# Linear attention and low-rank mixer on one core: k and v of three batches loaded through ScalarE's queue, alpha and q through SyncE's

## The chip, the cores and the metric

One core of a Trainium2 chip. The metric is the device time of one execution in microseconds. A run is called fast or slow by its own kernel's fastest run: slow is more than 1.5% above it. "SP" is SyncE, "PE" TensorE, "ACT" ScalarE, "DVE" VectorE, "POOL" GpSimd.

## The reference

```python
B, H, S, D = 4, 8, 768, 48
for t in range(S):                      # gated linear attention, per batch and head
    state = alpha[:, :, t, :, None] * state + einsum('bhd,bhe->bhde', k[:, :, t], v[:, :, t])
    y[:, :, t] = einsum('bhd,bhde->bhe', q[:, :, t], state)
x = y.transpose(0, 2, 1, 3).reshape(B, S, 384)
u = x + (x^T @ U @ V)^T                 # mixing over the sequence, rank 32
out = u + relu(u @ w_ch1) @ w_ch2       # 384 -> 1536 -> 384
```

## The kernel before

The kernel is written as a list of operations. A small planner in the kernel's own source (`Plan`) gives each an engine, a cost and a priority, plays the engines forward in time with those costs, and emits every engine's instructions in the order found. Each engine's order is fixed when the program is built. The costs of the plan thus shape the program, but not the chip.

Each batch loads alpha, k, q and v (1.18 MB each, rows of 192 bytes) into six buffers `io`. Sequence chunks of 128 are scanned in pairs: logarithm and cumulated sum of alpha (`lt`, L418 to L425), exponentials `ai` and `aa`, the multiplies `rk` (k, POOL) and `rq` (q, DVE), their transposes `kt` and `qt`, scores (L480), state (L512, L522) and result (L554, L559). For batches 2 and 3 the transposes are DMA transposes issued by SP. Then come the mixer and the two large products (L656, L678), which fill PE between the scans.

```python
def load(b):                                        # cut to the loads of b > 0
    ts = [Buf(io) for _ in range(4)]
    for n, (t, src) in enumerate(zip(ts, (alpha, k, q, v))):
        ...
        op = P.add("SP", 4250, lambda t=t, src=src: nc.sync.dma_start(t()[:, :, 0:D], ...),
                   prio=b + n / 10, hold=800.0, descs=385, late=(0.0, 0.0, 1500.0, 3000.0)[b], ...)
...
# transposes of batches 2 and 3
P.add("SP", 1000, lambda ...: nc.sync.dma_start_transpose(dst()..., src()...), ..., hold=1250.0, land=1300.0, descs=66, late=500.0)
...
# stores
P.add("SP", 550, lambda: nc.sync.dma_start(out[b, c * C : (c + 1) * C, :], ou()), ..., slack=4500.0 if b < 3 else None)
```

The planner's picture of SP (cut from `Plan.run`). Its figures, `RING` = 512 and 850 ns among them, are assumptions of the plan:

```python
free = t
for s, f, n in ring:                                # the plan's limit on queued transfers
    x = sum(m for s2, f2, m in ring if s2 >= s) + op.descs - RING
    if x > 0:
        free = max(free, s + (f - s) * min(1.0, x / n))
clock[eng] = free + op.hold
s = max(dma, clock[eng] + 850.0)                    # the plan's start, 850 ns after the issue
dma = s + op.cost
```

In the plan and in the texts below, "ring" stands for a queue of transfers as the trace lists them: q1 for what SP issues, q10 for what ScalarE issues.

Of the kernel before, what the change touches and what calls it, by code (L numbers as in the profile page):

```python
# [47 lines left out]


RING = 512  # L50
FCOST = 512 / 2.4 + 3.0


class Op:
    __slots__ = ("eng", "cost", "fn", "prio", "deps", "bufs", "n", "end", "users", "est", "i", "hold", "land", "descs", "dma", "slack", "port", "late")


class Plan:
# [9 lines left out]
        self.kinds = {}  # L68
        self.fill, self.fill_fn, self.fill_end, self.banks = None, None, None, ()

    def add(self, eng, cost, fn, r=(), w=(), prio=0.0, after=(), kind=None, hold=450.0, land=550.0, descs=40, dma=None, slack=None, port=False, late=0.0):
        op = Op()
        op.eng, op.cost, op.fn, op.prio = eng, cost, fn, prio
        op.i, op.hold, op.land, op.descs = len(self.ops), hold, land, descs
        op.port, op.late = port, late
        op.dma, op.slack = dma, (self.SLACK if eng == "SP" else 0.0) if slack is None else slack
        op.deps, op.users, op.est, op.end = set(), [], 0.0, None
        for k in r:
            d = self.writer.get(k)
            if d is not None:  # L80
                op.deps.add(d)
        for k in w:
            d = self.writer.get(k)
            if d is not None:
                op.deps.add(d)
            op.deps.update(self.readers.get(k, ()))
        for k in r:
            self.readers.setdefault(k, []).append(op)
        for k in w:
            self.writer[k] = op  # L90
            self.readers[k] = []
        op.deps.update(x for x in after if x is not None)
        if kind is not None:
            if kind in self.kinds:
                op.deps.add(self.kinds[kind])
            self.kinds[kind] = op
        op.deps.discard(op)
        op.bufs = []
        for k in list(r) + list(w):
            b = k[0] if isinstance(k, tuple) else k  # L100
            if isinstance(b, Buf) and b not in op.bufs:
                op.bufs.append(b)
        for b in op.bufs:
            b.left += 1
        self.ops.append(op)
        return op

    def run(self):
# [8 lines left out]
        clock = {"POOL": 1800.0}  # L117
        order = []
        dma = 0.0
        ring = []  # L120
# [3 lines left out]
        while todo:  # L124
            best = None
            for eng, cand in ready.items():
                now = clock.get(eng, 0.0)
                ok = []
                for op in cand:
                    t = op.est  # L130
                    for b in op.bufs:
                        if b.slot is None:
                            s = [f for f in map(b.pool.when, range(len(b.pool.slots))) if f is not None]
                            if not s:
                                t = None
                                break
                            t = max(t, min(s))
                    if t is not None:
                        ok.append((max(t, now), op))
                if not ok:  # L140
                    continue
                t0 = min(t for t, _ in ok)
                t1, op = min(((t, o) for t, o in ok if t <= t0 + 1.0), key=lambda x: (x[1].prio, x[1].i))
                if best is None or t1 < best[0]:
                    best = (t1, eng, op)
            if best is None:
                raise RuntimeError("the plan is stuck")
            t, eng, op = best
# [11 lines left out]
            for b in op.bufs:  # L160
                if b.slot is None:
                    p = b.pool
# [4 lines left out]
            if eng == "SP":  # L167
                free = t
                for s, f, n in ring:
                    x = sum(m for s2, f2, m in ring if s2 >= s) + op.descs - RING  # L170
                    if x > 0:
                        free = max(free, s + (f - s) * min(1.0, x / n))
                clock[eng] = free + op.hold
                s = max(dma, clock[eng] + 850.0)
                dma = s + op.cost
                ring.append((s, dma, op.descs))
                del ring[:-24]
                op.end = dma + op.land
            else:
                other = {"DVE": "POOL", "POOL": "DVE"}.get(eng)  # L180
                if op.port and last.get(other) is not None and last[other].port and clock[other] > t + 150.0:
                    op.cost *= 1.75 if eng == "DVE" else 1.2
                if eng in last:
                    last[eng] = op
                clock[eng] = t + op.cost
                op.end = t + op.cost
                if op.dma is not None:
                    s = max(dma, clock[eng] + 850.0)
                    dma = s + op.dma
                    op.end = dma + op.land  # L190
            order.append((t, op))
# [5 lines left out]
            for u in op.users:  # L197
                u.n -= 1
                lat = 0.0 if u.eng == eng and eng == "PE" else self.LAT[eng]
# [16 lines left out]
def kernel(  # L216
# [12 lines left out]
    nc = tc.nc  # L229
    B, H, S, D = q.shape  # L230
    C = 128
    NC = S // C
# [5 lines left out]
    NCT = DM // 128  # L238
# [10 lines left out]
    P = Plan()  # L249
# [50 lines left out]
    late = banks((0,), (1,), (2,), (3,))  # L300
# [60 lines left out]
    marks = {}  # L361

    def load(b):
        ts = [Buf(io) for _ in range(4)]
        for n, (t, src) in enumerate(zip(ts, (alpha, k, q, v))):
            if b == 0 and n == 2:
                marks["gate"] = P.add("POOL", 36 * 48 * 1.07 + 60, lambda t=t: nc.gpsimd.tensor_copy(t()[:, 0:36, 0:D], ts[0]()[:, 0:36, 0:D]), r=[(ts[0], c) for c in range(NC)], w=[(t, c) for c in range(NC)], prio=2)
            if b == 0 and n in (2, 3):
                for c in range(NC):
                    op = P.add("SP", 950, lambda t=t, src=src, c=c: nc.sync.dma_start(t()[:, :, 0:D].rearrange("p (h c) d -> p c h d", c=NC)[:, c], src[0, :, c * C : (c + 1) * C].rearrange("h p d -> p h d")), w=[(t, c)], prio=0.2 + ({2: (0, 1, 2), 3: (3, 4, 5)})[n][c // 2] / 100 + c / 1000, hold=350.0, descs=65, after=[marks["gate"]], slack=0.0)  # L370
            elif b == 0 and n == 1:
                gate = P.add("POOL", 40 * 48 * 0.9, lambda t=t: nc.gpsimd.memset(t()[:, 0:40, 0:D], 0.0), w=[(t, c) for c in range(NC)], prio=0)
                P.add("ACT", 870, lambda t=t, src=src: nc.scalar.dma_start(t()[:, :, 0:D], src[b].rearrange("h (c p) d -> p (h c) d", p=C)), w=[(t, c) for c in range(NC)], prio=0, after=[gate], dma=4100.0)
            else:
                op = P.add("SP", 4250, lambda t=t, src=src: nc.sync.dma_start(t()[:, :, 0:D], src[b].rearrange("h (c p) d -> p (h c) d", p=C)), w=[(t, c) for c in range(NC)], prio=b + n / 10, hold=800.0, descs=385, after=[marks.get("gate")], late=(0.0, 0.0, 1500.0, 3000.0)[b])
        return ts

    def stage_gla(b, g, sprev, xb, ins):
        kk = b * (NC // G) + g
        pr = 1000 + kk * 10  # L380
# [30 lines left out]
        for i0, n in parts:  # L411
            e = on(ev, i0)
# [29 lines left out]
        for eng, dst, src, fac in ((ek, rk, kt, ai), (eq, rq, qt, aa)):  # L442
            for i0, n in parts if dst is rq else [(0, G)]:
                e = on(eng, i0)
# [13 lines left out]
        both = lambda t: [(t, i) for i in range(G)]  # L458
        for src, dst, eng in ((rk, kT, ekt), (rq, qT, eqt)):
            if b in (2,3):  # L460
                P.add("SP", 1000, lambda src=src, dst=dst: nc.sync.dma_start_transpose(dst().rearrange("p g e c -> p (g e) c"), src().rearrange("t g h w -> t (g h w)")), r=both(src), w=both(dst), prio=pr / 1000 - 1, hold=1250.0, land=1300.0, descs=66, late=500.0)  # L461
                continue
            tb = Buf(gen)
            for i0, n in parts if src is rq else [(0, G)]:
# [120 lines left out]
    def stage_mix(b, xb, uT):  # L585
        pr = 500 + b * 10
# [36 lines left out]
        for c in range(NC):  # L623
# [2 lines left out]
            P.add("DVE", 550, lambda c=c, hb=hb: nc.vector.tensor_tensor(xb()[:, c, :], xb()[:, c, :], hb()[:, 0, 0:DM], op=ALU.add), r=[hb, (xb, c)], w=[(xb, c)], prio=pr)  # L626
            if b in (2,3):
                if c % 3 == 2:
                    P.add("SP", 1100, lambda c=c: nc.sync.dma_start_transpose(uT()[:, c - 2 : c + 1].rearrange("p c j t -> p (c j) t"), xb()[:, c - 2 : c + 1, :].rearrange("p c m -> p (c m)")), r=[(xb, c - i) for i in range(3)], w=[(uT, c // 3, j) for j in range(NCT)], prio=pr / 1000 - 1, hold=1300.0, land=1300.0, descs=66, late=500.0)
                continue  # L630
            if c % 2 == 1:
                ub2 = Buf(gen)
# [38 lines left out]
    def mlp2(b, xb, h1, c, utx):  # L671
# [14 lines left out]
        ou = Buf(outs)  # L686
        P.add("DVE", 550, lambda: nc.vector.tensor_tensor(ou(), xb()[:, c, :], hb()[:, 0, 0:DM], op=ALU.add), r=[hb, (xb, c)], w=[ou], prio=100)  # L687
        if (("SP",)*4)[b] == "SP":
            P.add("SP", 550, lambda: nc.sync.dma_start(out[b, c * C : (c + 1) * C, :], ou()), r=[ou], prio=-1, land=1700.0, slack=4500.0 if b < 3 else None)  # L689
        elif (("SP",)*4)[b] == "POOL":  # L690
            P.add("POOL", 550, lambda: nc.gpsimd.dma_start(out[b, c * C : (c + 1) * C, :], ou()), r=[ou], prio=50, land=2500.0, dma=550.0, slack=4500.0)
        else:
            P.add("ACT", 250, lambda: nc.scalar.dma_start(out[b, c * C : (c + 1) * C, :], ou()), r=[ou], prio=50, land=1700.0, dma=550.0, slack=4500.0)

    P.fill, P.banks = ((0.85, 250.0), (0.6, 700.0)), space
    P.fill_fn = lambda i: nc.tensor.matmul(ps[:, i, 0:512], lhsT=ident, rhs=fill_in, start=True, stop=True)  # L696
# [45 lines left out]
```

## Time and profile before

| | before |
|---|---|
| median of its first three runs | 174.87 us (174.59 to 177.56) |
| span of the profiled run | 173.6 us |
| PE busy, by the page | 157.6 us, so 16.0 us idle |
| of it idle from 30 to 62, and from 62 to 126 us | 0.24 and 8.96 us |
| half-speed spells of PE before the end | one, 3.4 us |
| packets on SP's queue (q1) and ScalarE's (q10) | 31.46 and 1.18 MB |

The idle times are lengths of stretches less PE's busy time in them. A half-speed spell comes from the trace's record of granted clock. It is counted here as half its length, 1.7 us for 3.4, an estimate. Fillers are products without use that keep PE busy. The mean granted clock is 0.987.

The lines themselves are in the prediction below. A timeline line reads: start, length, engine, source line, operation, written tile <- read tile, count, and in brackets the idle time before it with what ended it. "SPq" and "ACTq" lines are DMA issues, whose length is how long the issuing engine was held.

### The profile page before, as it was taken

Reading aid. Unit: us, or ns where it says so; the run is one execution under the profiler, and the core shown is the slowest. Engines: PE = TensorE matmul, PEld = TensorE weight load, DVE = VectorE, ACT = ScalarE, POOL = GpSimd, SP = SyncE. Lnnn points to the kernel's source line nnn. Section 1 sums busy time; section 2 is a strip of 40 time slices with the busy share of each in tenths; the row PEclk is TensorE's granted clock in tenths of the full one; section 3 lists DMA queues with packets and bytes.
Section 4 is the critical chain, followed back from the end, with each engine's and each line's share of the span. In section 5 each row is a group of like instructions: output and inputs, shape, how many; then the busy total and the mean of one; then the engine's idle time right before and its main releaser. Section 6 shows DMA issues by size and latency. Waiting matters only on the chain.

```text
span 173.6 us, 3909 instructions
## 1 busy us (share of the span) xinstructions
PE 157.6 (91%) x1632; PEld 96.3 (55%) x1632; DVE 89.8 (52%) x142; ACT 82.4 (47%) x147; POOL 53.9 (31%) x59
## 2 busy tenths in 40 slices
PE   5997999999999998998766899979799999999992
PEld 2445676556666675665344556536456556656650
DVE  2009991635266823398246128757948643544421
ACT  3296465688848576771533694024342210523200
POOL 8817745507942803247022062800000000000000
PEclk9999999999999999999998799999999999999998
DMA  3999999899998976998986989799400822101122
GB/s 103 274 288 209 192 265 384 254 267 311 372 260 238 260 204 194 251 288 251 208 196 164 251 253 262 187 227 205 124 4 0 186 86 93 46 0 45 54 87 91
DMA packets 58850, 33.14 MB, mean 191 GB/s; under 512 B 31440, under 2 KB 57680, under 8 KB 58832
## 3 DMA queue, kind: packets, MB, share of 16 engines
q1 hardware_dynamic: 56304, 31.46, 66.5%
q10 hardware_dynamic: 1552, 1.18, 2.3%
q0 software_dynamic: 976, 0.25, 1.4%
q8 instruction: 13, 0.21, 0.5%
q14 instruction: 5, 0.04, 0.1%
HBM read 24.08 MB, written 4.72 MB: 166 GB/s over the span
## 4 chain that ended last, share of the span: by engine, by line
PE 50%; DMA 32%; DVE 5%; SPq 5%; POOL 3%; ACT 2%; issue 1%; POOLq 0%; DVEq 0%; ACTq 0%
PE ps L678 19%; PE ps L656 17%; DMA io<-in_v_dram 10%; DMA qt<-rq 8%; DMA io<-in_alpha_dram 7%; DMA io<-in_k_dram 5%; SPq L689 3%; PE ps L451 3%; DVE pm L490 3%; PE ps L480 2%; DMA uT<-xb 2%; PE ps L559 2%; PE ps L696 2%; POOL rv L316 1%; SPq L461 1%
## 5 line engine op out<-in xcount | busy, mean ns | idle before, releaser
L678 PE MATMUL ps<-w_sb,h1t 128*128 128x384 bf16 x288 | 55.2, 326 | 0.0
L656 PE MATMUL ps<-uT,w_sb 128*128 128x384 bf16 x288 | 52.9, 328 | 1.2 <-DMA uT<-xb 1.2
L667 ACT ACTIVATE h1t<-ps 128x384 bf16<-128x384 f32 x48 | 23.5, 492 | 41.2 <-PE ps L656 41.0
L669 DVE TENSOR_SCALAR h1t<-ps 128x384 bf16<-128x384 f32 x48 | 26.3, 555 | 31.1 <-PE ps L656 30.3
L656 PEld LDWEIGHTS <-w_sb 128*128 128x128 bf16 x288 | 27.6, 98 | 18.9 <-DMA uT<-xb 1.5
L678 PEld LDWEIGHTS <-h1t 128*128 128x128 bf16 x288 | 27.5, 98 | 17.8 <-issue 0.6
L440 POOL TENSOR_TENSOR rk<-io,ai 128x768 bf16<-128x768 f32 x10 | 17.3, 1735 | 34.5 <-ACT ai L433 28.0
L490 DVE TENSOR_TENSOR pm<-ps,ut_ones 128x1024 bf16<-128x1024 f32 x18 | 21.6, 1220 | 8.7 <-PE ps L480 8.7
L687 DVE TENSOR_TENSOR ou<-xb,ps 128x384 f32<-128x384 bf16 x24 | 13.3, 553 | 19.9 <-PE ps L678 9.5
L696 PE MATMUL ps<-ones,ident 128*128 128x512 bf16 x52 | 14.5, 416 | 1.9 <-DVE rk L271 1.9
L440 DVE TENSOR_TENSOR rq<-io,aa 128x768 bf16<-128x768 f32 (+1 forms) x11 | 13.1, 1210 | 2.4 <-ACT aa L434 2.3
L575 ACT CAST xb<-ps 128x768 bf16<-128x768 f32 (+1 forms) x15 | 10.0, 672 | 8.0 <-PE ps L559 6.9
L316 POOL CAST rv<-io 128x768 bf16<-128x768 f32 (+1 forms) x11 | 9.7, 910 | 8.0 <-DMA io<-in_v_dram 8.0
L409 ACT ACTIVATE lt<-io 128x768 bf16<-128x768 f32 x12 | 9.8, 843 | 4.3 <-DMA io<-in_alpha_dram 4.0
L433 ACT ACTIVATE ai<-ps 128x768 bf16<-128x768 f32 x12 | 9.8, 817 | 2.7 <-PE ps L420 1.5
L316 POOL CAST w_sb<-io 128x768 bf16<-128x768 f32 x12 | 9.5, 825 | 4.3 <-DMA io<-in_moe_w_ch_dram 4.3
L480 PE MATMUL ps<-qt,kt 48*128 48x128 bf16 x192 | 8.7, 220 | 1.8 <-DMA qt<-rq 1.7
L434 ACT ACTIVATE aa<-ps 128x768 bf16<-128x768 f32 x12 | 9.9, 829 | 0.0
L356 POOL TENSOR_SCALAR_AFFINE_SELECT pm<-pm 128x1024 bf16<-128x1024 bf16 x6 | 6.5, 1092 | 11.0 <-DVE pm L490 8.5
L497 ACT CAST pm<-ps 128x1024 bf16<-128x1024 f32 x6 | 6.0, 1017 | 8.0 <-PE ps L480 8.0
L696 PEld LDWEIGHTS <-ident 128*128 128x128 bf16 x52 | 5.2, 105 | 7.7 <-issue 2.2
L559 PE MATMUL ps<-rv,pm 128*128 128x48 bf16 x192 | 8.5, 187 | 0.9 <-DVE pm L490 0.9
(64 smaller groups left out, 139.3 us busy)
## 6 DMA issues: line engine op xcount, KB each, us to landing
io<-in_moe_w_ch_dram SPq DMA_DIRECT2D x6, 768.0 KB, 7.4
out_dram<-ou SPq DMA_DIRECT2D x24, 192.0 KB, 2.3
io<-in_q_dram SPq DMA_DIRECT2D x6, 192.0 KB, 4.1
io<-in_v_dram SPq DMA_DIRECT2D x6, 192.0 KB, 3.8
vm_sb<-in_moe_V_dram POOLq DMA_DIRECT2D x4, 48.0 KB, 5.8
kt<-rk SPq DMA_TRANSPOSE x6, 2.8
qt<-rq SPq DMA_TRANSPOSE x6, 2.8
io<-in_alpha_dram SPq DMA_DIRECT2D x4, 0.2 KB, 8.6
```

The lines of the kernel that those rows point to most:

```text
L316: ENG[eng].tensor_copy(dst, src)
L440: ENG[eng].tensor_tensor(dst()[:, i0 : i0 + n, :, 0:D], ch(src, i0, n), fac()[:, i0 : i0 + n].rearrange("t g (h d) -> t g h d", d=D), op=A ...
L480: nc.tensor.matmul(s2[:, par, p, :], lhsT=kT()[o : o + D, i, p, :], rhs=qT()[o : o + D, i, p, :], start=(p == 0), stop=(p == HP - 1),)
L490: nc.vector.tensor_tensor(pmi().rearrange("t two hp c -> t (two hp) c"), sc().rearrange("p two (hp c) -> p (two hp) c", c=C), maskc.to_bro ...
L559: nc.tensor.matmul(y2[:, par, p, :], lhsT=pm[i]()[:, par, p, :], rhs=rv()[:, i, 2 * p + par, :], start=s0, stop=s1, skip_group_check=True,)
L575: nc.scalar.copy(x3, y3)
L656: nc.tensor.matmul(hb()[:, 0, 0:TW], lhsT=w1_sb[:, ct, jt * 128 : (jt + 1) * 128], rhs=uT()[:, 3 * tt : 3 * tt + 3, ct, :], start=(ct == 0 ...
L667: P.add("ACT", 500, lambda jt=jt, hb=hb: nc.scalar.activation(h1()[:, jt, :], hb()[:, 0, 0:TW], AF.Relu), r=[hb], w=[(h1, jt)], prio=100)
L669: P.add("DVE", 560, lambda jt=jt, hb=hb: nc.vector.tensor_scalar_max(h1()[:, jt, :], hb()[:, 0, 0:TW], 0.0), r=[hb], w=[(h1, jt)], prio=100)
L678: nc.tensor.matmul(hb()[:, 0, 0:DM], lhsT=h1()[:, jt, (c % 3) * C : (c % 3 + 1) * C], rhs=w2_sb[:, jt, :], start=(jt == 0), stop=(jt == NJ ...
L687: P.add("DVE", 550, lambda: nc.vector.tensor_tensor(ou(), xb()[:, c, :], hb()[:, 0, 0:DM], op=ALU.add), r=[hb, (xb, c)], w=[ou], prio=100)
L696: P.fill_fn = lambda i: nc.tensor.matmul(ps[:, i, 0:512], lhsT=ident, rhs=fill_in, start=True, stop=True)
```

## The change

The intent: SP carries loads, transposes and stores in one queue in the order of their issue, and a load issued soon behind another was seen to hold everything behind it (k of batch 1, issued at 24.66, held SP for 9.45 us; alpha, issued before it at 23.43, landed at 35.43). k and v of batches 1 to 3 go to ScalarE's queue. The planner is given new figures, estimates: 1800 ns from issue to first packet of a load for 850 (1.48 us for q at 66.70 and 1.52 us for v at 102.79 in the trace of the kernel before), SP held until 72% of the last large load has run (v of batch 1 held it until 49.07, 74% of the time from q's first packet at 45.84 to its last at 50.23), 1360 ns for a transpose's issue (1.24 to 1.86 us in that trace). Loads are chained (`pre`), and a ScalarE load may be planned at the earliest 4500 ns (`LEAD`) before the DMA engines are due to be free.

```diff
+LEAD = 4500.0
@@ Plan.run, choice of the next operation
-                    t = op.est
+                    if op.pre is not None and op.pre.end is None:
+                        continue
+                    t = max(op.est, dma - LEAD) if eng == "ACT" and op.dma is not None else op.est
@@ Plan.run, SP
                 clock[eng] = free + op.hold
-                s = max(dma, clock[eng] + 850.0)
+                if ring and ring[-1][2] > 300:
+                    clock[eng] = max(clock[eng], ring[-1][0] + 0.72 * (ring[-1][1] - ring[-1][0]))
+                s = max(dma, clock[eng] + op.lat)
@@ load
+            elif n in ((),(1,3),(1,3),(1,3))[b]:
+                marks["load"] = P.add("ACT", 870, lambda ...: nc.scalar.dma_start(...), ..., dma=4000.0, lat=1800.0, slack=300.0, late=..., pre=marks["load"])
             else:
-                op = P.add("SP", 4250, ..., hold=800.0, descs=385, ...)
+                marks["load"] = P.add("SP", 4000, ..., hold=800.0, descs=385, ..., lat=1800.0, pre=marks.get("load") if b else None)
@@ transposes: cost 1000 or 1100 -> 1250, hold 1250 or 1300 -> 1360 or 1380
@@ stores: slack 4500 -> 3000 for b < 3, lat 1450
```

More of the change, by code (lines that the diff above doesn't have):

```diff
@@ L50 @@
 RING = 512
+LEAD = 4500.0
 FCOST = 512 / 2.4 + 3.0
 class Op:
-    __slots__ = ("eng", "cost", "fn", "prio", "deps", "bufs", "n", "end", "users", "est", "i", "hold", "land", "descs", "dma", "slack", "port", "late")
+    __slots__ = ("eng", "cost", "fn", "prio", "deps", "bufs", "n", "end", "users", "est", "i", "hold", "land", "descs", "dma", "slack", "port", "late", "lat", "pre")
 class Plan:
@@ L69, in __init__, with add @@
         self.fill, self.fill_fn, self.fill_end, self.banks = None, None, None, ()
-    def add(self, eng, cost, fn, r=(), w=(), prio=0.0, after=(), kind=None, hold=450.0, land=550.0, descs=40, dma=None, slack=None, port=False, late=0.0):
+    def add(self, eng, cost, fn, r=(), w=(), prio=0.0, after=(), kind=None, hold=450.0, land=550.0, descs=40, dma=None, slack=None, port=False, late=0.0, lat=850.0, pre=None):
         op = Op()
@@ L74, in add @@
         op.i, op.hold, op.land, op.descs = len(self.ops), hold, land, descs
-        op.port, op.late = port, late
+        op.port, op.late, op.lat = port, late, lat
+        op.pre = pre
         op.dma, op.slack = dma, (self.SLACK if eng == "SP" else 0.0) if slack is None else slack
@@ L187, in run @@
                 if op.dma is not None:
-                    s = max(dma, clock[eng] + 850.0)
+                    s = max(dma, clock[eng] + op.lat)
                     dma = s + op.dma
@@ L373, in load @@
                 P.add("ACT", 870, lambda t=t, src=src: nc.scalar.dma_start(t()[:, :, 0:D], src[b].rearrange("h (c p) d -> p (h c) d", p=C)), w=[(t, c) for c in range(NC)], prio=0, after=[gate], dma=4100.0)
+            elif n in ((),(1,3),(1,3),(1,3))[b]:
+                marks["load"] = P.add("ACT", 870, lambda t=t, src=src: nc.scalar.dma_start(t()[:, :, 0:D], src[b].rearrange("h (c p) d -> p (h c) d", p=C)), w=[(t, c) for c in range(NC)], prio=b + n / 10, dma=4000.0, lat=1800.0, slack=300.0, late=(0.0, 0.0, 1500.0, 3000.0)[b], pre=marks["load"])
             else:
-                op = P.add("SP", 4250, lambda t=t, src=src: nc.sync.dma_start(t()[:, :, 0:D], src[b].rearrange("h (c p) d -> p (h c) d", p=C)), w=[(t, c) for c in range(NC)], prio=b + n / 10, hold=800.0, descs=385, after=[marks.get("gate")], late=(0.0, 0.0, 1500.0, 3000.0)[b])
+                marks["load"] = P.add("SP", 4000, lambda t=t, src=src: nc.sync.dma_start(t()[:, :, 0:D], src[b].rearrange("h (c p) d -> p (h c) d", p=C)), w=[(t, c) for c in range(NC)], prio=b + n / 10, hold=800.0, descs=385, after=[marks.get("gate")], late=(0.0, 0.0, 1500.0, 3000.0)[b], lat=1800.0, pre=marks.get("load") if b else None)
         return ts
@@ L460, in stage_gla @@
             if b in (2,3):
-                P.add("SP", 1000, lambda src=src, dst=dst: nc.sync.dma_start_transpose(dst().rearrange("p g e c -> p (g e) c"), src().rearrange("t g h w -> t (g h w)")), r=both(src), w=both(dst), prio=pr / 1000 - 1, hold=1250.0, land=1300.0, descs=66, late=500.0)
+                P.add("SP", 1250, lambda src=src, dst=dst: nc.sync.dma_start_transpose(dst().rearrange("p g e c -> p (g e) c"), src().rearrange("t g h w -> t (g h w)")), r=both(src), w=both(dst), prio=pr / 1000 - 1, hold=1360.0, land=1300.0, descs=66, late=500.0)
                 continue
@@ L628, in stage_mix @@
                 if c % 3 == 2:
-                    P.add("SP", 1100, lambda c=c: nc.sync.dma_start_transpose(uT()[:, c - 2 : c + 1].rearrange("p c j t -> p (c j) t"), xb()[:, c - 2 : c + 1, :].rearrange("p c m -> p (c m)")), r=[(xb, c - i) for i in range(3)], w=[(uT, c // 3, j) for j in range(NCT)], prio=pr / 1000 - 1, hold=1300.0, land=1300.0, descs=66, late=500.0)
+                    P.add("SP", 1250, lambda c=c: nc.sync.dma_start_transpose(uT()[:, c - 2 : c + 1].rearrange("p c j t -> p (c j) t"), xb()[:, c - 2 : c + 1, :].rearrange("p c m -> p (c m)")), r=[(xb, c - i) for i in range(3)], w=[(uT, c // 3, j) for j in range(NCT)], prio=pr / 1000 - 1, hold=1380.0, land=1300.0, descs=66, late=500.0)
                 continue
@@ L688, in mlp2 @@
         if (("SP",)*4)[b] == "SP":
-            P.add("SP", 550, lambda: nc.sync.dma_start(out[b, c * C : (c + 1) * C, :], ou()), r=[ou], prio=-1, land=1700.0, slack=4500.0 if b < 3 else None)
+            P.add("SP", 550, lambda: nc.sync.dma_start(out[b, c * C : (c + 1) * C, :], ou()), r=[ou], prio=-1, land=1700.0, slack=3000.0 if b < 3 else None, lat=1450.0)
         elif (("SP",)*4)[b] == "POOL":
-            P.add("POOL", 550, lambda: nc.gpsimd.dma_start(out[b, c * C : (c + 1) * C, :], ou()), r=[ou], prio=50, land=2500.0, dma=550.0, slack=4500.0)
+            P.add("POOL", 550, lambda: nc.gpsimd.dma_start(out[b, c * C : (c + 1) * C, :], ou()), r=[ou], prio=50, land=2500.0, dma=550.0, slack=3000.0)
         else:
-            P.add("ACT", 250, lambda: nc.scalar.dma_start(out[b, c * C : (c + 1) * C, :], ou()), r=[ou], prio=50, land=1700.0, dma=550.0, slack=4500.0)
+            P.add("ACT", 250, lambda: nc.scalar.dma_start(out[b, c * C : (c + 1) * C, :], ou()), r=[ou], prio=50, land=1700.0, dma=550.0, slack=3000.0)
     P.fill, P.banks = ((0.85, 250.0), (0.6, 700.0)), space
```

## The prediction

> **What bounds the kernel now.** I read the page first, then the busy time by stretch, then TensorE's timeline for its gaps, then the sync engine's own timeline for what caused them.
>
> From the page: busy times, the slices of TensorE and of the DMA engines, the chain that ended last.
>
> ```profile
> PE 157.6 (91%) x1632; PEld 96.3 (55%) x1632; DVE 89.8 (52%) x142; ACT 82.4 (47%) x147; POOL 53.9 (31%) x59
> ...
> PE   5997999999999998998766899979799999999992
> ...
> PE 50%; DMA 32%; DVE 5%; SPq 5%; POOL 3%; ACT 2%; issue 1%; POOLq 0%; DVEq 0%; ACTq 0%
> ```
>
> TensorE is busy for 91% of the span, so the kernel can only gain where TensorE is idle, throttled, or runs fillers (52 warm-up products, L696). The busy time by stretch says where that is (columns: stretch, its length, then the busy time of PE, PEld, DVE, ACT and POOL, granted clock, DMA share, GB/s):
>
> ```profile
> 30.00:62.00 32.00, 31.76 (x353) 20.57 (x351) 17.84 (x28) 23.24 (x39) 16.82 (x18) 1.00 0.93 282
> 62.00:85.50 23.50, 22.41 (x205) 13.68 (x202) 12.79 (x20) 15.41 (x30) 8.00 (x6) 1.00 0.82 228
> 85.50:126.00 40.50, 32.63 (x471) 20.30 (x470) 23.86 (x35) 16.90 (x31) 10.52 (x8) 0.96 0.85 209
> 126.00:170.30 44.30, 44.23 (x286) 26.16 (x281) 20.75 (x39) 10.47 (x21) 0.00 (x0) 1.00 0.21 63
> ```
>
> TensorE is full from 30 to 62 us and from 126 to the end. It loses 23.50 - 22.41 = 1.09 us in the second row and 40.50 - 32.63 = 7.87 us in the third. The third row also has a clock of 0.96: the trace's clock record has one half-speed spell of 3.4 us there, just after a long gap, worth about 1.7 us of work. Recoverable: 1.09 + 7.87 + 1.7 = about **10.7 us**. TensorE's timeline names the largest gaps:
>
> ```profile
> 87.90 0.27 PE L554 MATMUL ps<-st,qt 48*128 48x48 bf16 x8 [2.20 <-DMA qt<-rq]
> ...
> 93.43 0.40 PE L480 MATMUL ps<-qt,kt 48*128 48x128 bf16 x8 [1.67 <-DMA qt<-rq]
> ```
>
> It waits for the DMA transposes of batch 2's q (qt). Why they are late stands in the sync engine's own timeline (start, length, what):
>
> ```profile
> 54.49 4.06 SPq L375 DMA_DIRECT2D io<-in_k_dram  x1
> 58.65 7.83 SPq L689 DMA_DIRECT2D out_dram<-ou  x3
> 66.70 0.71 SPq L375 DMA_DIRECT2D io<-in_q_dram  x1
> 67.86 4.34 SPq L375 DMA_DIRECT2D io<-in_v_dram  x1
> 72.30 4.48 SPq L689 DMA_DIRECT2D out_dram<-ou  x1
> 76.99 0.70 SPq L375 DMA_DIRECT2D io<-in_alpha_dram  x1
> 77.79 4.62 SPq L689 DMA_DIRECT2D out_dram<-ou  x1
> 82.51 1.86 SPq L461 DMA_TRANSPOSE kt<-rk  x1
> ```
>
> One in-order queue carries everything. A load issued behind a queued load takes 4 us or more (9.45 us at 24.66) where a free one takes 0.7[...]. Stores pay too. So batch 2's q is issued at 66.70 and lands at 73.5 (issue to landing 6.8 us); VectorE's multiply for qt starts at 73.64, which the waits put down to ScalarE but which is this landing. The first transpose is issued at 82.51, although its rk was done at 69.2. The same queue holds batch 3's k until 92.23 and its v until 102.79 (landing at 110.0).
>
> [...] the issues blocked for 4 to 9 us against about 3.8 us of packets per load. [...] batch 0's k, the one load from ScalarE, went through a queue of its own (q10) and its issue took 0.83 us at 4.37 us, while SP's alpha load (issued 0.87, landed about 7.7) was in flight. [...]
>
> **The change, part by part**, with the order of instructions in both builds.
>
> 1. *Six loads (k, v of batches 1 to 3) leave SP.* There they held it for 9.45 + 8.03 + 4.06 + 4.34 + 0.71 + 0.73 = 27.3 us. On ScalarE each costs about 0.85 us (0.83 measured): 5.1 us on an engine busy 47%, in one spot each, mostly beside TensorE work buffered in eight PSUM banks. I count 0.5 us for it. As each ScalarE load comes 8 us or more after its last one, I expect little blocking in its ring.
>
> 2. *Batch 2's q and alpha of batch 3 move up.* q is now issued after two stores instead of after k and three stores. alpha of batch 2 should be through by 56, so q goes out near 55 and lands near 64, not 73.5; v (ScalarE, near 65) lands near 71, not 78.1. The qt multiply then waits only for its exponential (68 to 69). Six transposes at 1.25 to 1.36 us an issue run from about 71 to 80, the last landing near 83, against 93.3 before. The new TensorE order also puts about 12 more products of 0.163 us (2 us) in front of the first L554, so TensorE gets there near 88. The 2.20 + 0.20 + 0.45 + 1.67 = 4.5 us of gaps go, and the half-speed spell (1.7). The 0.55 us wait for v goes too.
>
> 3. *Batch 3* (gaps after 95 us: 7.87 - 4.5 = 3.4): its k is issued near 77 instead of 92, its v near 91 instead of 103, and SP's transposes no longer stand behind a store blocked for 5.01 us (103.62). I give back half: 1.7 us.
>
> Sum of gains: 4.5 + 1.7 + 0.55 + 1.7 = about 8.4 us.
>
> 4. *Losses, early.* Before, alpha, k and the three w2 loads followed each other in one ring: alpha landed at 35.43, k at 39.86. alpha is on the path: L418 at 36.36 waited 0.17 us for its logarithm. Now k starts near 34 on its own ring and takes turns with alpha's last packets (0.5 us lost), then with w2. A load has 96 packets of 768 B per DMA engine, the w2 loads together 96 of 1536 B; alone a load takes 3.8 us and the w2s 5.9, so k, in turns with w2, may last until 43, 3 us later. Its multiply (1.64) is followed by a transpose that TensorE reached at 44.56, with a slack of 2.9 us, and GpSimd's casts of w2 come behind it. I put this at 2 us (0 to 4).
>
> 5. *Three more fillers at the start* (26 for 23[...]): L418 at 8.54 slips by up to 0.64 us, and ScalarE's exponentials with it. I count 0.4.
>
> 6. *Latencies in the plan* (1800 for 850 ns to start a load, SP held by a queued load, transposes held 1360 for 1250) are no work, but move the order nearer to what SP does. Their gain is in 2 and 3.
>
> Net: -8.4 + 0.5 + 0.5 + 2 + 0.4 = **-5.0 us**, so 174.87 - 5.0 = 169.9.
>
> **Rivals.**
> (a) *Early contention eats the gain.* k of batch 1 late, GpSimd late, w2's casts late: 3 to 6 us lost between 36 and 50, and a gap there could bring its own half-speed spell. For it: the packet arithmetic of step 4. Against it: 2.9 us of slack, and the first w2 casts now go ahead of the multiplies. Time 172 to 175.
> (b) *ScalarE blocks.* If its issue stalls as SP's does when its last load is still draining, 4 us on ScalarE would stop the evacuation of PSUM. For it: SP's 4 to 9 us. Against it: the 0.83 us issue and the spacing. Time 173 to 177.
> (c) *The transposes share with ScalarE's loads.* They were alone in SP's ring, landing 2.8 us after issue; in turns with k or v of batch 3 that may be 5 us. The 5 us won in step 2 hides it in batch 2; batch 3 could keep its gaps. Time 171 to 172.
> (d) *All gaps go.* Then 10.7 instead of 8.4 us and small losses: 165 to 166, near the floor for this much TensorE work.
>
> **Range and chances.** Centre 169.9; the early loss can be 2 us less or 4 more, and the late gaps 2 us either way, so 166.5 to 174.0. The mark for faster is 174.87 / 1.02 = 171.4. The centre lies 1.5 us beyond it, with a spread of about 2.8 us, and rivals (a) and (c) end on the other side: faster 0.64, same 0.32, slower 0.04.
>
> **What the new profile would show.** Steps 1 and 2: DMA issues of about 0.85 us on ScalarE, q10 with seven loads of 1.18 MB, 8.3 MB, where it had one, the first transpose near 71 and no gap over 1 us before L554 of batch 2, clock 1.00 throughout the middle. Step 3: v of batch 3 landing before 100. Step 4: the multiply rk of batch 1 starting after 42 on GpSimd, and TensorE gaps between 36 and 50 where there were none. I would be wrong if those early gaps sum to over 5 us, if a ScalarE issue takes 3 us or more, or if the qt gaps stay.

## The result, and the profile after

Four runs of each: 168.53 us median (167.06 to 169.94) against 175.57 us (174.59 to 177.56). The ratio of the fast runs is 0.954, with a 95% interval from 0.942 to 0.967. Ratios here are fast runs over fast runs of the same rounds, so not quite the ratio of the medians quoted. In later rounds (x7, on chip 13) it was 0.949 (0.944 to 0.954).

From the page of the changed kernel, the busy times, the granted clock by slices, the queues (packets, MB, share of 16 engines), and the chain of work that ended last:

```profile
span 165.7 us, 3925 instructions
...
PE 156.9 (95%) x1635; PEld 96.0 (58%) x1635; DVE 89.9 (54%) x142; ACT 82.5 (50%) x153; POOL 54.0 (33%) x59
...
PEclk9999999999999999999999999999999999999999
...
q1 hardware_dynamic: 46992, 24.38, 56.2%
q10 hardware_dynamic: 10864, 8.26, 17.9%
...
PE 67%; DMA 10%; SPq 8%; issue 7%; POOL 4%; DVE 1%; ACT 1%; ACTq 0%; POOLq 0%
```

PE does the same work in 7.9 us less span, at full clock throughout, and 7.08 MB went over to q10. In the chain that ended last DMA is 10% of the span, for 32% before. The busy time by stretch of the changed kernel (columns as in the prediction):

```profile
30.00:62.00 32.00, 31.22 (x323) 19.73 (x321) 15.12 (x26) 23.32 (x42) 17.49 (x18) 1.00 1.05 321
62.00:85.50 23.50, 23.27 (x244) 14.69 (x241) 15.46 (x22) 15.29 (x32) 8.05 (x6) 1.00 1.09 267
85.50:126.00 40.50, 38.95 (x530) 24.54 (x529) 28.93 (x43) 20.11 (x38) 10.10 (x8) 1.00 0.71 165
```

Idle from 62 to 126 us fell from 8.96 to 0.23 + 1.55 = 1.78 us: 7.2 us gained. The spell that cost 1.7 us is gone. Against that, idle from 30 to 62 us rose by 0.54, and the fillers, 55 for 52, were busy 15.4 us for 14.5, of which 0.6 us filled idle time before 30 us (2.84 for 3.45). 7.2 + 1.7 - 0.5 - 0.9 + 0.6 = 8.1 us, against 7.9 measured. DMA share and GB/s in the first two rows are higher than before (1.05 for 0.93, 1.09 for 0.82), which fits loads that are done earlier.

PE's timeline has no wait for qt any more. What is left in batch 2 is one wait for a masked score:

```profile
91.81 0.37 PE L567 MATMUL ps<-rv,pm 128*128 128x48 bf16 x8 [1.07 <-DVE pm L498]
```

SP's timeline of the changed kernel, which answers to the one in the prediction:

```profile
24.77 11.16 SPq L344 DMA_DIRECT2D io<-in_moe_w_ch_dram  x3
...
56.01 1.00 SPq L383 DMA_DIRECT2D io<-in_q_dram  x1
57.06 9.02 SPq L697 DMA_DIRECT2D out_dram<-ou  x2
66.29 0.71 SPq L383 DMA_DIRECT2D io<-in_alpha_dram  x1
67.09 8.89 SPq L697 DMA_DIRECT2D out_dram<-ou  x2
76.08 1.71 SPq L469 DMA_TRANSPOSE kt<-rk  x1
77.91 3.52 SPq L469 DMA_TRANSPOSE qt<-rq  x1
...
86.45 1.26 SPq L469 DMA_TRANSPOSE qt<-rq  x1
```

q of batch 2 is issued at 56.01 for 66.70, alpha of batch 3 at 66.29 for 76.99, the first transpose at 76.08 for 82.51. SP is still held for long (8.89 us by two stores behind a load), but what it holds up is no longer late for PE. ScalarE's issues are short, here the first two:

```profile
32.36 0.70 ACTq L381 DMA_DIRECT2D io<-in_k_dram  x1
44.53 0.70 ACTq L381 DMA_DIRECT2D io<-in_v_dram  x1
```

### The profile page after: what moved, and what is told of

It reads as the page before. It is cut to its first block, busy times and chain, and to the rows that moved or that the text cites.

```text
span 165.7 us, 3925 instructions
## 1 busy us (share of the span) xinstructions
PE 156.9 (95%) x1635; PEld 96.0 (58%) x1635; DVE 89.9 (54%) x142; ACT 82.5 (50%) x153; POOL 54.0 (33%) x59
## 4 chain that ended last, share of the span: by engine, by line
PE 67%; DMA 10%; SPq 8%; issue 7%; POOL 4%; DVE 1%; ACT 1%; ACTq 0%; POOLq 0%
PE ps L686 28%; PE ps L664 21%; SPq L376 7%; DMA io<-in_moe_w_ch_dram 6%; DMA io<-in_alpha_dram 4%; PE ps L567 2%; PE ps L488 2%; POOL rk L448 2%; PE ps L520 2%; POOL w_sb L322 2%; PE ps L459 2%; PE ps L693 1%; PE ps L633 1%; PE ps L562 1%; POOL io L373 1%
## 5 line engine op out<-in xcount | busy, mean ns | idle before, releaser
L664 PE MATMUL ps<-uT,w_sb 128*128 128x384 bf16 x288 | 52.2, 326 | 0.3 <-ACT xb L583 0.3
L664 PEld LDWEIGHTS <-w_sb 128*128 128x128 bf16 x288 | 27.7, 98 | 17.9 <-issue 0.5
L704 PE MATMUL ps<-ones,ident 128*128 128x512 bf16 x55 | 15.4, 422 | 1.9 <-DVE rk L277 1.9
L567 PEld LDWEIGHTS <-pm 128*128 128x128 bf16 x192 | 7.1, 96 | 3.6 <-DVE pm L498 1.6
```

The lines of the kernel that those rows point to most:

```text
L567: nc.tensor.matmul(y2[:, par, p, :], lhsT=pm[i]()[:, par, p, :], rhs=rv()[:, i, 2 * p + par, :], start=s0, stop=s1, skip_group_check=True,)
L664: nc.tensor.matmul(hb()[:, 0, 0:TW], lhsT=w1_sb[:, ct, jt * 128 : (jt + 1) * 128], rhs=uT()[:, 3 * tt : 3 * tt + 3, ct, :], start=(ct == 0 ...
L704: P.fill_fn = lambda i: nc.tensor.matmul(ps[:, i, 0:512], lhsT=ident, rhs=fill_in, start=True, stop=True)
```

## The experiments

Two things changed together: the queue of six loads, and the order of all engines' work. Theory A says that the gain is SP's freed time. Rival B says that it is the truer plan and the order it makes. As the order is fixed when the program is built, each can be had alone: the loads can be issued from the other queue at their place in the list, everything else untouched.

This table sums up what the profiles show; idle times in us as defined above, spells in us at half speed before the end.

| kernel | ratio to before (95%) | idle 30 to 62 | idle 62 to 126 | spells |
|---|---|---|---|---|
| before | 1 | 0.24 | 8.96 | 3.4 |
| changed | 0.954 (0.942 to 0.967) | 0.78 | 1.78 | none |
| x1_before_act | 0.996 (0.989 to 1.004) | 4.34 | 2.95 | 3.4 + 3.4 |
| x2_after_sp | 1.010 (1.002 to 1.018) | 1.02 | 7.25 | 3.4 + 3.4 |
| x3_model_only | 0.997 (0.991 to 1.003) | 0.02 | 5.62 | 3.4 |
| x4_before_warm | 0.992 (0.985 to 0.998) | 0.39 | 7.32 | none |
| x5_five_on_act | 0.992 (0.985 to 0.998) | 3.84 | 2.98 | 6.8 |
| x6_k1_early | 0.978 (0.971 to 0.984) | 3.23 | 1.78 | 3.4 |
| x7_after_again | 0.949 (0.944 to 0.954) | 0.81 | 1.78 | none |
| x8_k3_late | 0.985 (0.980 to 0.990) | 1.49 | 5.14 | 10.2 |
| x9_fill23 | 0.946 (0.940 to 0.952) | 1.20 | 1.78 | none |
| x10_four_on_act | 0.991 (0.982 to 1.000) | 0.66 | 6.98 | 13.7 (profile of a slow run) |
| x11_k3_late_v3_sp | 0.951 (0.943 to 0.959) | 1.19 | 1.77 | 3.4 (profile of a slow run) |
| x12_best | 0.951 (0.943 to 0.960) | 0.56 | 1.77 | 3.4 |

All gave correct results. The four or more runs of each kernel were compared with runs of before on the same chip.

### x1_before_act: the queue without the order

```diff
-nc.sync.dma_start(t()[:, :, 0:D], ...)          # before's load, b > 0
+(nc.scalar if b and n in (1, 3) else nc.sync).dma_start(t()[:, :, 0:D], ...)
```

> The order of all work is that of the kernel before on every engine; only the six loads of k and v (batches 1 to 3) are issued by ScalarE at the same place of the global order, and leave SP. Theory A (the gain is SP's freed time): most of the gain comes without any new order, ratio to before 0.96 to 0.975 (168 to 171 us), first transpose of batch 2 before 78 us. Rival B (the gain is the new order of the plan): within 1% of before, 173.5 to 176.5 us, TensorE again waits over 3 us for qt.

The time was that of before (175.59 us median, 175.83 before), so by time alone Theory A missed. But its mechanism is in the profile: the first transpose was issued at 76.14, PE did not wait for qt at all, and idle from 62 to 126 us fell from 8.96 to 2.95. That gain of 6.0 us was lost earlier, at one place of PE's timeline (second line):

```profile
76.14 1.71 SPq L461 DMA_TRANSPOSE kt<-rk  x1
...
41.05 0.32 PE L418 MATMUL ps<-lt,ut_ones 128*128 128x384 bf16 x1 [4.11 <-ACT lt L409]
```

PE waited 4.11 us for the logarithm of batch 1's alpha and then ran at half speed for 3.4 us. ScalarE had issued k of batch 1 at 23.66, SP its alpha at 24.41. The queues' packets in the stretch from 33 to 37 us of this run:

```profile
q1 hardware_dynamic: 865, 0.66, 56.9%
q10 hardware_dynamic: 773, 0.59, 50.1%
```

The two queues moved nearly as many packets each. alpha, needed at once, got about half of the packets, while the other half went to a k that had 3 us of slack before. alpha landed 15.7 us after its issue (at 40.1, for 35.4 before). 6.0 - 4.1 - 1.7 leaves 0.2 us, almost nothing, as measured. A second spell of 3.4 us, as before has one, stood at 96.3 (granted clock 0.96 from 85.5 to 126 us).

### x2_after_sp: the order without the queue

```diff
-nc.scalar.dma_start(t()[:, :, 0:D], ...)        # changed kernel's k and v, b > 0
+nc.sync.dma_start(t()[:, :, 0:D], ...)
```

> The order of all work is that of the changed kernel on every engine; only the six loads are issued by SP at the same place of the global order. Theory A: SP is held again by blocked issues, the transposes come late, ratio 0.99 to 1.02 (173 to 178 us). Rival B: it keeps the gain, ratio 0.95 to 0.965.

It was 1.0% slower than before: Rival B falls, and Theory A's side was met. PE waited for qt again (1.38, 0.42 and 1.67 us) and 2.70 us for a DVE that stood at a store's buffer. The first transpose was issued at 88.16, later than in either kernel:

```profile
88.16 1.35 SPq L469 DMA_TRANSPOSE kt<-rk  x1
...
99.33 0.62 PE L488 MATMUL ps<-qt,kt 48*128 48x128 bf16 x16 [1.67 <-DMA qt<-rq]
```

### x3_model_only: planned anew for SP alone

```diff
-            elif n in ((),(1,3),(1,3),(1,3))[b]:
+            elif n in ((),(),(),())[b]:
```

> The changed plan with all loads planned on and issued by SP, so the plan knows of SP's blocked issues and orders around them (73 fillers for 55). Theory A: little of the gain, ratio 0.985 to 1.01. Rival B (a truer model is enough): ratio 0.96 to 0.975.

The truer plan with all loads on SP is as before within its interval. It does order around SP's holds (idle from 62 to 126 us is 5.62 for 8.96), but 73 fillers for 52 take up the difference. The loads themselves are late: PE waited 1.50 and 1.44 us for v. So neither part alone gives the gain, and together they give 4.6 to 5%.

### x4_before_warm: what the half-speed spell costs

```diff
                 s2 = sc().rearrange("p two (hp c) -> p two hp c", c=C)
+                for _ in range(6 if (b, g, i) == (2, 2, 0) else 0):
+                    nc.tensor.matmul(sc()[:, 0, :], lhsT=ident, rhs=fill_in, start=True, stop=True)
```

> The kernel before with six filler products (1.3 us) put into the 1.67 us gap ahead of the last scores of batch 2, nothing else moved. If the half-speed spell of 3.4 us after that gap is a cost of its own of 1.7 us, the spell goes and the ratio is 0.985 to 0.993 (about 1.5 us less). If the spell hides beside other waits, or stays, the ratio is 0.997 to 1.003.

The spell went from the profile, and the ratio is 0.992, inside what was expected of a spell that costs its own 1.7 us. The interval is wide (0.985 to 0.998), but excludes no effect. The size of a spell's cost isn't shown by it. The fast runs of x4 have a mean clock of 0.997, those of before in the same rounds 0.973; counted at half its length, that difference alone would be some 4 us (an estimate: 0.024 of 176), and 1.5 was measured. Nor do the runs of before follow their clock: 175.83 us at 1.000, 175.16 at 0.961. The spells lasted 3.4, 6.8, 10.2 or 13.7 us (table above); what sets these lengths isn't shown. So some part of the gain, of unsure size, is not the waits, but the clock that they cost.

### x5_five_on_act and x6_k1_early: is it the overtaken alpha?

x5 is x1 with batch 1's k left on SP. x6 takes the changed kernel and moves one issue only, of the same k, from 32.4 to near 24 us.

```diff
# x5
+(nc.scalar if (b, n) in ((1, 3), (2, 1), (2, 3), (3, 1), (3, 3)) else nc.sync).dma_start(...)
# x6: before emission, in the changed kernel
+order: k of batch 1 placed ahead of the first state copy on ScalarE
```

> As the run with the order of before and six loads on ScalarE, but batch 1's k stays on SP behind alpha; the other five go through ScalarE. In the run with six, k of batch 1 was issued by ScalarE at 23.66 us, ahead of SP's alpha at 24.41, alpha landed at 40.1 instead of 35.4, TensorE waited 4.11 us for its logarithm and ran at half speed for 3.4 us. Theory A2 (the freed SP is worth about 4% but was cancelled by k overtaking alpha): alpha lands near 35.5, no 4 us gap, ratio 0.96 to 0.975. Rival B2 (the order of before can't use loads that come earlier): ratio 0.99 to 1.005.

> The changed kernel with one DMA issue moved: ScalarE issues batch 1's k near 23.5 us instead of 32.4; every other instruction keeps its place. A2: k is served before alpha, alpha lands 4 to 5 us later (near 40), TensorE gets a gap near 37 us of about 4 us and a half-speed spell, 4 to 6 us lost, ratio to before 0.975 to 0.99. Rival (rings share evenly, so alpha loses at most 1 to 2 us, and the rest is made up later): ratio 0.955 to 0.968.

x6 did what was expected of it: alpha landed near 40 (16.5 us after its issue at 23.54), a gap of 3.09 us opened at L430 (the L426 of the changed kernel), a 3.4 us spell came with it, and the ratio is 0.978, where the changed kernel had 0.954 and 0.949 in other rounds:

```profile
40.98 0.32 PE L430 MATMUL ps<-lt,ut_ones 128*128 128x384 bf16 x1 [3.09 <-ACT lt L421]
```

Idle from 62 to 126 us is 1.78 us as in the changed kernel: nothing of the loss was made up later. So the place of one ScalarE issue is worth about half of the gain. That k was issued at 24.14, 0.6 us after alpha, and from 33 to 37 us q1 moved 867 packets and q10 790: here a load shared evenly with one in the other queue without being issued first.

x5 missed its number: 0.992, not 0.960 to 0.975. alpha was in time (issued 24.15, landed 11.7 us later), and idle from 62 to 126 us was 2.98 as in x1. But the next load overtook something else:

```profile
49.14 0.48 PE L678 MATMUL ps<-w_sb,h1t 128*128 128x384 bf16 x2 [2.01 <-POOL w_sb L316]
49.92 1.22 PE L678 MATMUL ps<-w_sb,h1t 128*128 128x384 bf16 x5 [0.29 <-POOL w_sb L316]
52.23 2.72 PE L678 MATMUL ps<-w_sb,h1t 128*128 128x384 bf16 x8 [1.09 <-POOL w_sb L316]
```

PE waited 3.4 us for the casts of the second weight, beside whose loads batch 1's v, issued by ScalarE at 38.80, took about half of the packets (q1 481 and q10 509 from 41 to 44 us). Its spells lasted 6.8 us. Before, that v stood behind the weights in SP's queue (issued at 41.04, they from 34.15). 6.0 us gained, 3.6 us of waits and 1.7 us of clock lost: 0.7 us, of the 1.5 measured.

### x10_four_on_act: only batches 2 and 3 through ScalarE

```diff
+(nc.scalar if (b, n) in ((2, 1), (2, 3), (3, 1), (3, 3)) else nc.sync).dma_start(...)
```

> The order of before, with only batches 2 and 3's k and v issued by ScalarE; batch 1's k and v stay on SP, so nothing can overtake alpha or the w2 loads. With five on ScalarE, batch 1's v, issued at 38.80, was served ahead of w2, and TensorE waited 3.4 us for w2's casts and ran 6.8 us at half speed; from 62 us on that kernel idled 3.0 us where before idles 9.0. Theory A3 (two effects: freed SP gains some 5 to 7 us from 62 us on, overtaking costs it early): ratio 0.96 to 0.975, no gap over 1 us before 62 us. Rival C (the order of before gives the gain back later in any case): ratio 0.985 to 1.0.

No gap over 1 us is left before 62 us, as expected, but the ratio is 0.991: Theory A3's number fell and Rival C's range was met. The profile is of a slow run (178.55 us), so the sizes in it aren't used for the fast runs. In it, ScalarE issued batch 3's k at 85.52, in the middle of batch 2's six transposes:

```profile
85.83 1.44 SPq L461 DMA_TRANSPOSE kt<-rk  x1
87.37 4.49 SPq L461 DMA_TRANSPOSE qt<-rq  x1
```

The last transpose's issue took 4.49 us for 1.25, and PE waited 5.24 us for it. Whether the fast runs lose their time there too is open; it would be the same thing in a third place. Their mean clocks are 0.971, 0.971 and 0.980, so they weren't free of spells.

### x7, x8 and x11: ScalarE's queue, and whether the transposes still bind

In the changed kernel batch 2's first two transposes landed 7.9 and 7.0 us after issue, behind batch 3's k, which ScalarE issued at 72.55 (from 75 to 79 us q10 moved 1,445 packets, q1 194). x8 moves that k to 87 us, and x11 also moves batch 3's v from ScalarE to SP. x7 is the changed kernel again, in the same rounds as x8.

```diff
# x8: before emission, in the changed kernel
+order: k of batch 3 placed ahead of batch 2's first score copy on ScalarE
# x11: x8, and for v of batch 3
+(nc.sync if (b, n) == (3, 3) else nc.scalar).dma_start(...)
```

> The changed kernel once more, as the mark for the two runs beside it: ratio to before 0.95 to 0.96.

> The changed kernel with one DMA issue moved: ScalarE issues batch 3's k near 87 us instead of 72.55; nothing else moves. In the changed kernel it was served ahead of batch 2's first transposes, which landed 7.9 and 7.0 us after issue. Theory: those two land about 3 to 4 us after issue, some 3 us earlier, and nothing is gained, because TensorE only gets to them at 87 us: within 0.5% of the changed kernel. Rival (the transposes still bound batch 2): 0.8 us or more faster. A loss of up to 1 us would mean that batch 3's k then stands in the way of batch 3.

> The changed kernel with batch 3's k issued late (87 us) as in the run that lost, and batch 3's v moved from ScalarE to SP at the same place. In the run that lost, ScalarE's v issue at 89.95 lasted 5.40 us, TensorE then waited 3.17 us for ScalarE and ran 10.2 us at half speed. If that blocked issue on ScalarE is the whole loss: it goes, ratio to before 0.945 to 0.962, the transposes of batch 2 land about 3 us after issue and nothing is gained by that. If the late k itself was the loss: ratio 0.975 to 0.99.

x8 was 6 us slower than x7 (174.66 for 168.52 us median), which neither side had expected. The transposes came early, as intended (2.9 us to landing for the first, 2.9 to 4.4 for the early ones), and PE got to batch 2's scan with the same two gaps, 0.22 and 1.07 us. Then ScalarE stood still. Its timeline in x8:

```profile
87.43 0.70 ACTq L385 DMA_DIRECT2D io<-in_k_dram  x1
...
89.95 5.40 ACTq L385 DMA_DIRECT2D io<-in_v_dram  x1
...
95.39 0.80 ACT L587 CAST xb<-ps 128x768 bf16<-128x768 f32 x1 [4.85 <-issue]
```

v's issue came while a k issued 2.5 us earlier was still on its way (it landed 11.1 us after its issue), and held the engine for 5.40 us, with PE's results waiting in PSUM. PE then waited 3.17 us and ran for 10.2 us at half speed:

```profile
96.24 0.61 PE L492 MATMUL ps<-qt,kt 48*128 48x128 bf16 x8 [3.17 <-ACT xb L587]
```

x11 has the same late k and no second load on ScalarE: 0.951, level with x7. So the blocked issue was the whole loss. And as x11 isn't faster than the changed kernel although its transposes land at 2.9 to 4.5 us, they no longer bind there.

### x9_fill23 and x12_best: two attempts to do better

```diff
# x9 and x12: batch 0's alpha
-lat=1800.0
+lat=1800.0 if b else 850.0
# x12: GpSimd, before emission
+order: both casts of the first w2 load placed behind batch 1's first two rk
```

> The changed kernel with the start latency of batch 0's alpha in the plan back at 850 ns, which takes four fillers out ahead of the first product and moves nothing else. If the extra fillers delay the first batch, as TensorE's 0.56 us later start of L664 (31.23 for 30.67) suggests: 0.4 to 0.8 us faster than the changed kernel, ratio to it 0.995 to 0.998. Rival (the DMAs of batch 0 set this start, not the fillers): no difference.

> The changed kernel with four fillers fewer at the start and, on GpSimd, the two casts of the first w2 load moved from ahead of batch 1's first two rk to behind them, as k lands at about 40.5 and that w2 load at 41.65. The gap of 0.49 us for rk near 46.5 goes; with the fillers 0.5 to 1.0 us faster than the changed kernel, ratio to before 0.942 to 0.955. Rival (the slack is taken back elsewhere): as the changed kernel, within 0.2%.

x9's median is 167.82 us beside 168.52 of the changed kernel, its ratio 0.946 (0.940 to 0.952) beside 0.949 (0.944 to 0.954): it may be 0.3% faster, but the intervals overlap, so this is inconclusive. x12 closed its gap (no wait for rk is left in its profile; idle from 30 to 62 us 0.56 for 0.81), yet its ratio was 0.951. No version is shown to beat the changed kernel. In x12's profile the 1.07 us wait of batch 2 was followed by a half-speed spell; in those of the changed kernel, x7 and x9 the same wait was not. A spell, at up to 1.7 us, can hide what either edit gives.

## Why the prediction was right

The measured 168.53 us lies in the range of 166.5 to 174.0, and the change is faster by over 2%. By its own steps:

- **What bounds it** held: nearly all of the gain came from the stretch from 62 to 126 us, where PE had idled 8.96 us and lost 1.7 to the clock.
- **Step 1** held. Six issues of 0.69 to 0.70 us came to 4.2 us on ScalarE, for 5.1 worked out. That ScalarE doesn't block was right only for this spacing: x8 and x11 show that two loads 2.5 us apart cost 6 us, and in x1 an issue of v at 95.20, 5.8 us after that of k, took 3.40 us.
- **Step 2** had the right gain (4.5 us of qt waits and the spell) and a wrong timetable. q of batch 2 was issued at 56.01 (said: near 55), but landed at 66.9 (64), and v at 73.2 (71); the first transpose went out at 76.08 (71), as two stores held SP for 8.89 us; the last landed near 89.3, not 83. The qt waits went all the same. In the margin, PE reached its first use at 87.15 (said: near 88), and the last scores of batch 2 came at 92.12.
- **Step 3** was mis-sized, in the good direction: of batch 3's 3.4 us of gaps, half (1.7) was counted as gained, but all save some 0.5 went (1.55 us of idle is left from 85.5 to 126 us, 1.07 of it batch 2's wait for a masked score), so about 2.9. That new wait of 1.07 us, which no step foresaw, takes most of the surplus back. v of batch 3 landed at 100.8, not before 100.
- **Step 4** was mis-sized and its reason was wrong. 2 us was counted for batch 1's k taking turns with w2; the rise in idle is 0.54 us. k landed at 40.5, not 43. Batch 1's rk did start after 42 (43.22), as forecast, but for the casts ahead of it and not for k. Its 3.8 and 5.9 us are estimates (1.18 and 2.36 MB at the 316 and 400 GB/s that the trace of the kernel before shows from 70.8 to 72.3 and from 41.5 to 44.5 us come to 3.7 and 5.9). The w2 loads were not there to take turns with: SP's issue of them was held for 11.16 us (24.77 to 35.93) behind alpha in its own queue, so k ran first (packets from 33.88 to 40.02) and w2 came later. The first w2 load landed at 41.65, and POOL's casts of it, ordered ahead of rk, made the one new wait (0.49 us).
- **Step 5** (0.4 us; three fillers at the 0.216 us from start to start of the trace are 0.65 us) is in the timeline as a start of the first L664 at 31.23 for 30.67; x9 couldn't confirm it in time.
- **Rival (a)** is real, but in other kernels: x1, x5 and x6 are what it describes. The prediction counted the plan's new order in steps 2 and 3 only (step 6). x1, x5 and x6 show a worth that it didn't name: the order places batch 1's k and v where they take nothing from a load that is needed sooner. **Rival (b)** happened in x8 (5.40 us). **Rival (c)** happened (7.9 and 7.0 us to landing) and was hidden. **Rival (d)**, all gaps go, came near: 1.78 us of idle is left of 8.96.

The sum was -5.0 us: 8.4 gained, 3.4 lost. The span fell by 7.9, so the time lies in the range, but 1.4 us under its centre (169.9). The gains were close: idle from 62 to 126 us fell by 8.96 - 1.78 = 7.2 us, and with the spell's 1.7 that is 8.9. The losses were not: 8.9 - 7.9 leaves 1.0 us, about the 0.54 us of step 4 and the 0.56 us by which L664 starts later in step 5 (not shown to be lost time). So the term that was mis-sized most is step 4, 2 us for 0.54, and then step 1's and alpha's 0.5 us each, of which the profile shows nothing.

What stays open: why two loads on two queues shared packets evenly in x1, x5 and x6, but ran one after the other in the changed kernel (from 48.8 to 52 us, q10 moved 1,225 packets and q1 106, though SP's issue of alpha had ended at 47.9); why the changed kernel's runs fall on two levels (167.1 to 167.5 and 169.6 to 169.9 in its first rounds), for which a spell is a candidate (its slow runs have a mean clock of 1.00 and 0.99, so it can't explain the first; x7's one slow run has 0.989, its fast ones 0.998 to 1.000); and where x10's fast runs lose their time.

## What to carry to other kernels

The second DMA queue freed the first one's issuer (first transpose at 76.14 for 82.51 in x1), but also let a load overtake what used to stand safely ahead of it in one queue (alpha landed 15.7 us after its issue in x1, for 12.0 before): move loads to it only together with a rule for when each may be issued. On a compute engine, space the loads: issued 8.4 us or more after the last one they took 0.70 us each in the changed kernel, but 3.40 us when 5.8 us apart (x1) and 5.40 us when 2.5 us apart (x8), where PE then waited 3.17 us for ScalarE. And look for half-speed spells behind each gap of TensorE: by the estimate above one can more than double its price (in x12, 3.4 us at half speed, 1.7 us, after a wait of 1.07 us).

## What the runs show of the queues and the clock

- Time to issue: soon behind a load of 1.18 MB in 192-byte rows, a load's issue held SP for 4.06 to 9.45 us (before), those of three weight loads for 11.16 us (changed kernel), and one on ScalarE held it for 5.40 us (x8), against 0.71 us for q at 66.70 (before), with no load under way. Such a load took 4.39 us from its first packet to its last (q of batch 1, before).
- Sharing between queues: nearly even in x1 (865 and 773 packets in 4 us), but not in the changed kernel (106 and 1,225 packets in 3.2 us). Whether the quiet queue had packets ready then isn't shown, so these runs give no rule for it.
- Bandwidth: the DMA share from 62 to 85.5 us rose from 0.82 to 1.09 (x1, the queue alone: 1.04; x2, the order alone: 0.80), so the saved issue time was worth bandwidth in this stretch. Against that stand the waits behind a load in the other queue: 4.11 us in x1, 3.4 in x5 and 3.09 in x6, each followed by a half-speed spell.
- Spells of 3.4 us came after waits of 0.45 and 1.67 us close together (before), in x1 at 96.3 (where no wait but those of 4.11 us at 41.05 and 1.9 us for the first filler was over 0.6 us), and after one wait of 1.07 us in x11 and x12, but not after the same wait in the changed kernel, x7 and x9, nor after one of 1.7 us in x4. So these runs give no length of wait from which a spell follows.
